# Forgetting attention followed by a spectral mix on one core: the output stage's steps, its GpSimd blocks and its stores are reordered

## The chip, the core and the metric

The kernel runs on one core of one Trainium2 chip. The metric is the time of one execution on the device in microseconds (us), as the median of the runs; lower is better. Engines are named as the profile names them: PE is TensorE's matmul, PEld its weight load, DVE is VectorE, ACT is ScalarE, POOL is GpSimd, and SP is SyncE, whose queue issues the stores of the result.

## The reference

Eight batches, eight heads, 576 positions, 64 values a head, 64 spectral modes; all inputs and the result are float32.

```python
# attention with a forgetting gate
scores = q @ k.T / 8;  cum = cumsum(log(clip(f, 1e-4, 1)))
attn   = softmax(causal(scores + cum[:, :, :, None] - cum[:, :, None, :]))
x      = (attn @ v)            # regrouped to (8, 576, 512)
# spectral mix
X = rfft(x, axis=1)            # the first 64 modes are kept
Y[:, m] = X[:, m] @ (w_r[m] + 1j * w_i[m])     # 64 complex matrices of 512 x 512
y = irfft(Y, n=576, axis=1)
u = x + y
out = u + maximum(u @ w_ch, 0)                 # (8, 576, 512)
```

## The kernel before

**Stages.** The first stage runs the attention of 32 pairs of heads and transforms each pair into the frequency domain. The second stage streams the 64 pairs of mode matrices through TensorE in 16 groups of four modes and, between the transfers, prepares for every batch the product of `x` with `w_ch` (`XW`) and folds the first 48 modes into both `x_all` (which becomes the base of `u`) and `XW` (which becomes the base of `z = u @ w_ch`). The last stage, the output stage, is what the change touches. It starts when the last four modes are known.

**What the output stage makes.** The result has 8 batches of 576 rows, taken as four blocks of 128 rows and one of 64. Two batches form a pair `p`. A step makes two result blocks of 128 x 512 float32 (256 KB each), called n = 0 and n = 1 here. An ordinary step takes one block of 128 rows of both batches of a pair. The last 64 rows of the two batches of one pair fit together into one block of 128 rows, so a joined step makes the 64-row ends of two pairs, which are four batches. There are 16 ordinary and 2 joined steps, 36 blocks, 9.44 MB. The list `steps` (L647 to L651) gives the order: before, pair 0, the joined step of pairs 0 and 1, pair 1, pair 3, the joined step of pairs 2 and 3, pair 2. The joined steps are therefore numbers 4 and 13 of 0 to 17.

**One block.** `base` (L857) puts the prepared part into a bank of PSUM with one matmul by the identity per block (`base_mm`, L657): for U from `x_all`, for Z from `XW`. `rest` (L867) adds the last 16 modes of each batch with one short matmul per block (L877), from `yl`, which holds 32 rows for each of four batches. An ordinary matmul of `rest` uses 32 of the array's rows, a joined one 64. ACT copies U from PSUM to the tile `u_sb` (`copy_u`, L907 to L912). Then DVE makes the result block, `max(Z, 0) + u_sb`, in one instruction (L944).

**Help from GpSimd.** In the steps of `by_pool` the block n = 1 is not made on DVE: ACT writes `Relu(Z)` (L941) and GpSimd adds `u_sb` (L942). In the steps of `late_x` the matmul that puts `x_all` into U is left out for n = 1, and GpSimd adds `x_all` to the finished block (L949).

**The last modes.** `yl[h]` is made by `last_modes(h)` (L885 to L905) for batches 0 to 3 (h = 0, ahead of step 0) and 4 to 7 (h = 1): eight matmuls, then one copy on ACT (L904) and one on DVE (L905). `turn` is the iteration in whose beginning the second call stands. It also decides the banks: PSUM has eight, two in `psT`, two in `psA` and four in `psX`. Until the turn Z has `psX` and U changes between `psT` and `psA`; after it U has `psX` and Z changes between the other two. So each of U and Z is double buffered.

**The order in iteration i.** Instructions stand on each engine in the order of the program. PE has the base of U of step i + 1, the base of Z of step i, the `rest` of U of step i + 1 and the `rest` of Z of step i. ACT copies U of step i + 1. Then the two blocks of step i are made and stored.

**Stores.** The list `held` collects finished blocks, and SP issues them (L963), the last one appended first. Steps 0 to 7 and the last one are `alone`: each block is stored by itself, and where GpSimd works on n = 1, that store is held back until n = 0 of the next step has been made, and stands behind it. The other ordinary steps store both blocks in one transfer of 512 KB, when both are ready. A result tile `o_sb` holds the two blocks of a step; there are seven of them.

Of the kernel before, what the change touches and what calls it, by code (L numbers as in the profile page):

```python
# [13 lines left out]
ALU = mybir.AluOpType  # L14
ACT = mybir.ActivationFunctionType
# [8 lines left out]
def kernel(  # L24
# [11 lines left out]
    nc = tc.nc  # L36
# [586 lines left out]
    with ExitStack() as bctx:  # L623
# [15 lines left out]
        psT = bctx.enter_context(tc.tile_pool(name="psT", bufs=2, space=PSUM))  # L639
        psA = bctx.enter_context(tc.tile_pool(name="psA", bufs=2, space=PSUM))  # L640
        psX = bctx.enter_context(tc.tile_pool(name="psX", bufs=4, space=PSUM))

        def bank(where, name):
            return where.tile([128, D], F32, tag={id(psT): "t", id(psA): "a", id(psX): "x"}[id(where)], name=name)

        last64 = NSB - 1
        steps = []  # L647
        for p0, p1 in ((0, 1), (3, 2)):
            steps += [[(p0, sb), (p0, sb)] for sb in range(last64)]
            steps += [[(min(p0, p1), last64), (max(p0, p1), last64)]]  # L650
            steps += [[(p1, sb), (p1, sb)] for sb in range(last64)]  # L651

        def base_mm(ps, n, k, which, stop=False):

# [188 lines left out]
                            )  # L843

        usb = bctx.enter_context(tc.tile_pool(name="usb", bufs=6))
        by_pool = (2, 6, 9, 14)
        late_x = (3, 5, 7, 8, 10, 11, 12, 15, 16)
        turn = 7
        yl = {}

        def parts(n):
# [5 lines left out]
        def base(n, which):  # L857

            wide = n < turn if which else n > turn
            where = psX if wide else (psT, psA)[n % 2]  # L860
            ps = [bank(where, "UZ"[which]) for _ in range(2)]
            for k in range(2):
                if which or not k or n not in late_x:
                    base_mm(ps[k], n, k, which)
            return ps

        def rest(n, which, ps):  # L867

            for b, k, sb in parts(n):
                r = (b + 2 * which) % 4  # L870
                if sb < last64:
                    grp = slice(32 * r, 32 * r + 32)
                    lhsT = BI4[grp, sb * 128 : sb * 128 + 128]
                else:
                    grp = slice(32 * r, 32 * r + 64)
                    lhsT = BI4_il[grp, :, :].rearrange("p i j -> p (i j)")
                nc.tensor.matmul(  # L877
                    ps[k][:],
                    lhsT=lhsT,
                    rhs=yl[b // 4][which][grp, :],  # L880
                    start=bool(k) and not which and n in late_x,
                    stop=True,
                )

        def last_modes(h, py, pyw):  # L885

            for eb in range(NEB):
                nc.tensor.matmul(
                    py[:, eb * 128 : (eb + 1) * 128],
                    lhsT=YLa[h][:, eb, :, :].rearrange("p b c -> p (b c)"),  # L890
                    rhs=ident_bf[:, :],
                    start=True,
                    stop=True,
                )
            for eb in range(NEB):
                nc.tensor.matmul(
                    pyw[:],
                    lhsT=YLw[h][:, eb, :, :].rearrange("p b c -> p (b c)"),
                    rhs=wch[:, eb, :],
                    start=(eb == 0),  # L900
                    stop=(eb == NEB - 1),
                )
            yl[h] = [ylpool.tile([128, D], BF16, tag="yl", name="yl") for _ in range(2)]
            nc.scalar.copy(yl[h][0][:], py[:])  # L904
            nc.vector.tensor_copy(yl[h][1][:], pyw[:])  # L905

        def copy_u(n, U):  # L907

            us = [usb.tile([128, D], F32, tag="usb", name="u_sb") for _ in range(2)]
            for k in range(2):  # L910
                nc.scalar.copy(us[k][:], U[k][:])
            return us  # L912
# [5 lines left out]
        u_next = copy_u(0, U0)  # L918
        held = []
        for i in range(len(steps)):  # L920
            if i == turn:
                last_modes(1, bank(psT, "pyl"), bank(psT, "pywl"))
            more = i + 1 < len(steps)
            if more:
                U = U1 if i == 0 else base(i + 1, 0)
            Z = Z0 if i == 0 else base(i, 1)
            if more:
                rest(i + 1, 0, U)
            rest(i, 1, Z)
            u_now = u_next  # L930
            if more:
                u_next = copy_u(i + 1, U)
            o_sb = wpool.tile([128, 2, D], F32, tag="w8", name="o_sb")
            p, sb = steps[i][0]
            s0 = sb * 128
            split, late = i in by_pool, i in late_x
            alone = i < 8 or i == len(steps) - 1
            for n in range(2):
                u_sb = u_now[n]
                if split and n == 1:  # L940
                    nc.scalar.activation(o_sb[:, n, :], Z[n][:], ACT.Relu)  # L941
                    nc.gpsimd.tensor_tensor(o_sb[:, n, :], o_sb[:, n, :], u_sb[:], ALU.add)  # L942
                else:
                    nc.vector.scalar_tensor_tensor(  # L944
                        o_sb[:, n, :], Z[n][:], 0.0, u_sb[:], ALU.max, ALU.add
                    )
                if late and n == 1:
                    ov = o_sb[:, n, :].rearrange("p (g c) -> p g c", g=NEB)
                    nc.gpsimd.tensor_tensor(ov, ov, x_all[:, :, 2 * p + n, sb, :], ALU.add)  # L949
                if sb == last64:  # L950
                    b0 = 2 * steps[i][n][0]
                    held.append((out[b0 : b0 + 2, s0:S, :].rearrange("b p e -> p b e"), o_sb[:, n, :]))
                elif alone:
                    held.append((out[2 * p + n, s0 : s0 + 128, :], o_sb[:, n, :]))
                elif n == 1:
                    held.append(
                        (out[2 * p : 2 * p + 2, s0 : s0 + 128, :].rearrange("b p e -> p b e"), o_sb[:])
                    )
                if alone and n == 1 and (split or late):
                    break  # L960
                while held:
                    to, frm = held.pop()
                    nc.sync.dma_start(to, frm)  # L963
# [30 lines left out]
```

## Time and profile before

| | |
|---|---|
| median of 3 runs | 437.77 us (437.42 to 439.06) |
| profiled execution, time | 440.27 us |
| profiled execution, span from first to last instruction | 438.5 us |
| granted TensorE clock, mean over the span | 0.938 |
| output stage, from its first store's issue to the last instruction | 408.99 to 438.5 us |
| stores | 20 of 256 KB and 8 of 512 KB |

The span is what the profile's views show; 1.77 us of the profiled execution lie outside it. Each row of a group or of the timeline names the line of the kernel, the engine, the operation and `out<-in` with shapes. In the view of stretches each row gives the length, the busy time of the five engines with their instruction counts, the granted clock, the mean busy share of the 16 DMA engines and what they moved in GB/s. In the view of waits a row gives the waiting queue, what released it, the total, the count and the longest wait.

### The profile page before, as it was taken

The page shows a single profiled execution, that of the slowest core. Times are in us where ns is not written, and L with a number is a line of the kernel's source. Part 1 is how long each engine was busy: PE and PEld are TensorE (multiplying, and loading weights), DVE is VectorE, ACT ScalarE, POOL GpSimd, SP SyncE. Part 2 cuts the span into 40 slices and gives each one's busy share as a digit, 9 for nine tenths or more (in the row PEclk, how much of TensorE's full clock was granted, in tenths as well). Part 3 has the DMA queues.
Part 4 walks back from the last instruction along what each step waited for, and adds up shares of the span by engine and source line. Part 5 has one row for each costly group of instructions (what it writes and reads, how often), then busy time and mean ns, then how long its engine had stood idle before and what let it go on. Part 6 is the DMA issues. An engine that isn't in the chain of part 4 may idle for free.

```text
span 438.5 us, 10295 instructions
## 1 busy us (share of the span) xinstructions
PE 348.4 (79%) x4264; PEld 191.7 (44%) x4274; DVE 268.0 (61%) x650; ACT 234.8 (54%) x359; POOL 146.1 (33%) x216
## 2 busy tenths in 40 slices
PE   1589877798988988989896484699888598889993
PEld 0355555555555555555563242243333233335330
DVE  4677888867788778888885231222233166455784
ACT  4455776777877756566561022034132166355883
POOL 6454444444544444344214111111122212100283
PEclk9999999999999999999999588599699599699998
DMA  8999999999999999999999999999999999995598
GB/s 180 205 232 221 230 222 232 228 230 228 230 231 224 228 223 227 224 224 223 230 215 212 212 212 212 213 211 212 212 211 212 210 209 210 210 210 106 193 341 331
DMA packets 68414, 96.75 MB, mean 221 GB/s; under 512 B 3600, under 2 KB 45072, under 8 KB 68368
## 3 DMA queue, kind: packets, MB, share of 16 engines
q0 software_dynamic: 62800, 85.64, 105.5%
q1 hardware_dynamic: 5568, 10.47, 6.6%
q8 instruction: 33, 0.54, 0.5%
q14 instruction: 13, 0.11, 0.1%
HBM read 163.73 MB, written 9.44 MB: 395 GB/s over the span
## 4 chain that ended last, share of the span: by engine, by line
PE 40%; DMA 32%; DVE 19%; ACT 3%; issue 3%; POOL 1%; POOLq 0%; ACTq 0%; DVEq 0%
DMA w<-in_moe_w_i_dram 22%; DMA w<-in_moe_w_r_dram 8%; PE pav L477 6%; DVE vT L384 5%; DVE qkT L360 5%; PE A L194 5%; DVE x_all L492 4%; PE pd L521 4%; PE sps L432 4%; PE tv L382 3%; PE vp L393 3%; DMA qk<-in_k_dram 2%; PE U L657 2%; PE s L423 2%; ACT e L426 2%
## 5 line engine op out<-in xcount | busy, mean ns | idle before, releaser
L439 ACT ACTIVATE et<-sps 128x1024 bf16<-128x1024 f32 x96 | 96.0, 1049 | 15.8 <-PE sps L432 12.8
L477 PE MATMUL pav<-vs,et 128*128 128x65 bf16 (+1 forms) x896 | 52.7, 200 | 0.2 <-DVE vn L372 0.2
L360 DVE COPY qkT<-tp 128x640 bf16<-128x640 bf16 x64 | 48.8, 764 | 4.8 <-PE tp L355 4.7
L818 DVE TENSOR_TENSOR Yb<-A,yx 128x512 bf16<-128x512 f32 x15 | 10.4, 691 | 61.6 <-PE A L194 61.6
L477 PEld LDWEIGHTS <-et 128*128 128x128 bf16 (+1 forms) x896 | 37.6, 104 | 18.2 <-issue 13.7
L432 PE MATMUL sps<-qkT 64*128 64x512 bf16 (+4 forms) x320 | 40.3, 315 | 1.1 <-DVE qkT L360 1.1
L697 PE MATMUL pxw<-wch,xT 128*128 128x512 bf16 (+1 forms) x152 | 39.5, 405 | 1.0 <-DVE xT L687 0.4
L194 PE MATMUL A<-w,XP 128*16 128x512 bf16 (+1 forms) x240 | 22.2, 453 | 21.8 <-DMA w<-in_moe_w_i_dram 14.1
L355 PE MATMUL tp<-ident_bf,qk 128*64 128x128 bf16 x576 | 30.6, 238 | 10.9 <-DMA qk<-in_k_dram 10.9
L492 DVE TENSOR_TENSOR x_all<-pav,rcp 128x384 bf16<-128x384 f32 (+2 forms) x96 | 36.2, 377 | 3.3
L384 DVE COPY vT<-tv 128x576 bf16<-128x576 bf16 x32 | 24.2, 757 | 19.7 <-PE tv L382 19.7
L165 POOL DMA_DIRECT2D w<-in_moe_w_r_dram x16 | 11.9, 742 | 70.6 <-PE A L194 50.8
L156 POOL DMA_DIRECT2D w<-in_moe_w_r_dram x27 | 20.4, 757 | 39.9 <-PE A L194 9.1
L704 ACT CAST XW<-pxw 128x512 bf16<-128x512 f32 (+1 forms) x16 | 9.3, 584 | 45.6 <-PE pxw L697 26.6
L404 ACT COPY vs<-vp 128x576 bf16<-128x576 bf16 x32 | 20.5, 639 | 21.9 <-PE vp L400 21.9
L704 ACT CAST yx<-pxw 128x512 bf16<-128x512 f32 (+1 forms) x24 | 14.0, 584 | 32.8 <-PE pxw L697 32.8
L109 POOL DMA_DIRECT2D qk<-in_q_dram x32 | 19.5, 611 | 35.1 <-DMA w<-in_moe_w_r_dram 8.4
L165 POOL DMA_DIRECT2D w<-in_moe_w_i_dram x19 | 13.3, 697 | 52.4 <-PE A L194 23.8
L744 ACT CAST x_all<-pu 128x512 bf16<-128x512 f32 (+1 forms) x40 | 23.4, 584 | 10.6 <-PE pu L743 9.8
L491 DVE RECIPROCAL rcp<-pav 128x6 f32<-128x6 f32 (+2 forms) x96 | 16.2, 169 | 17.7 <-PE pav L477 17.6
L156 POOL DMA_DIRECT2D w<-in_moe_w_i_dram x27 | 20.3, 752 | 18.5 <-DMA w<-in_moe_w_i_dram 8.0
L355 PEld LDWEIGHTS <-qk 128*64 128x64 bf16 x576 | 19.7, 117 | 14.8 <-issue 9.6
(149 smaller groups left out, 685.3 us busy)
## 6 DMA issues: line engine op xcount, KB each, us to landing
w<-in_moe_w_r_dram POOLq DMA_DIRECT2D x16, 1024.0 KB, 29.8
w<-in_moe_w_i_dram POOLq DMA_DIRECT2D x15, 1024.0 KB, 32.4
w<-in_moe_w_r_dram POOLq DMA_DIRECT2D x27, 512.0 KB, 10.9
w<-in_moe_w_i_dram POOLq DMA_DIRECT2D x27, 512.0 KB, 12.4
vt<-in_v_dram POOLq DMA_DIRECT2D x29, 288.0 KB, 10.6
out_dram<-o_sb SPq DMA_DIRECT2D x20, 256.0 KB, 3.2
qk<-in_q_dram POOLq DMA_DIRECT2D x32, 144.0 KB, 10.8
qk<-in_k_dram POOLq DMA_DIRECT2D x32, 144.0 KB, 10.6
```

The lines of the kernel that those rows point to most:

```text
L156: nc.gpsimd.dma_start(w8[:, t, :, :], src[4 * u : 4 * u + 4, dc * 128 : (dc + 1) * 128, :].rearrange("m p e -> p m e"),)
L165: nc.gpsimd.dma_start(w8[:, j : j + step, :, :].rearrange("p m r e -> p m (r e)"), src[m : m + step, 256:512, :].rearrange("m (p r) e -> p ...
L194: nc.tensor.matmul(A[32 * j : 32 * j + M, :], lhsT=lhsT, rhs=rhs, start=st_, stop=sp_)
L355: nc.tensor.transpose(tp[64 * hp : 64 * hp + 64, r - r0, :, :].rearrange("p n c -> p (n c)"), qk[:, hp, r * 64 : r * 64 + 64], ident_bf[:, :],
L360: nc.vector.tensor_copy(st[i]["T"][:].rearrange("p n (c r) -> p n c r", r=9)[:, :, :, r0:r1], tp[:, 0 : r1 - r0, :, :].rearrange("p r n c ...
L384: nc.vector.tensor_copy(st[i]["vT"][:].rearrange("p (c r) -> p c r", r=9), tv[:].rearrange("p r c -> p c r"))
L432: nc.tensor.matmul(ps[:, hp, c : c + n], lhsT=KT[sl, jb * 128 : jb * 128 + 128], rhs=QT[sl, i0 : i0 + n], start=True, stop=True,)
L439: nc.scalar.activation(st[i]["et"][:, T, :, :], ps[:], ACT.Exp, scale=scale)
L477: nc.tensor.matmul(pav[:Ms, sb % 3, hp, :], lhsT=eblk(i, hp, jb, sb), rhs=rhs, start=(jb == 0), stop=(jb == sb),)
L492: nc.vector.tensor_tensor(x_all[:ns, g, b, lo:hi, :].rearrange("p s (h d) -> p s h d", h=2), pav[:ns, lo % 3 : lo % 3 + n, :, 0:Dh], _stri ...
L697: nc.tensor.matmul(pxw[rows, :], lhsT=xT[:, eb, sb * 128 : sb * 128 + Ms], rhs=wch[:, eb, :], start=(eb == 0), stop=(eb == NEB - 1),)
L744: nc.scalar.copy(x_all[rows, :, to, sb, :], pu[rows, :].rearrange("p (g c) -> p g c", g=NEB))
```

## The change

The joined steps move from numbers 4 and 13 to the two ends, 0 and 17. The pairs between them keep their order (0, 1, 3, 2). GpSimd makes block n = 1 of three steps instead of four (2, 8 and 15 instead of 2, 6, 9 and 14), and there Relu comes ahead of the copies of the next U on ACT. `late_x` has nine steps as before, others in part. Every block is stored by itself in all steps, so there are 36 stores. The last modes of batches 4 to 7 are made at iteration 8 instead of 7, in the banks of `psA` instead of `psT`; step 9, the first that reads them, has its U in that same iteration.

```diff
-        steps = []
-        for p0, p1 in ((0, 1), (3, 2)):
-            steps += [[(p0, sb), (p0, sb)] for sb in range(last64)]
-            steps += [[(min(p0, p1), last64), (max(p0, p1), last64)]]
-            steps += [[(p1, sb), (p1, sb)] for sb in range(last64)]
+        steps = [[(p, sb), (p, sb)] for p in (0, 1, 3, 2) for sb in range(last64)]
+        steps = [[(0, last64), (1, last64)]] + steps + [[(2, last64), (3, last64)]]
...
-        by_pool = (2, 6, 9, 14)
-        late_x = (3, 5, 7, 8, 10, 11, 12, 15, 16)
-        turn = 7
+        by_pool = (2, 8, 15)
+        late_x = (3, 5, 6, 9, 10, 11, 12, 13, 14)
+        turn = 8
...
             if i == turn:
-                last_modes(1, bank(psT, "pyl"), bank(psT, "pywl"))
+                last_modes(1, bank(psA, "pyl"), bank(psA, "pywl"))
...
             u_now = u_next
-            if more:
-                u_next = copy_u(i + 1, U)
             o_sb = wpool.tile([128, 2, D], F32, tag="w8", name="o_sb")
             p, sb = steps[i][0]
             s0 = sb * 128
-            split, late = i in by_pool, i in late_x
-            alone = i < 8 or i == len(steps) - 1
+            if i in by_pool:
+                nc.scalar.activation(o_sb[:, 1, :], Z[1][:], ACT.Relu)
+                nc.gpsimd.tensor_tensor(o_sb[:, 1, :], o_sb[:, 1, :], u_now[1][:], ALU.add)
+            if more:
+                u_next = copy_u(i + 1, U)
             for n in range(2):
-                u_sb = u_now[n]
-                if split and n == 1:
-                    nc.scalar.activation(o_sb[:, n, :], Z[n][:], ACT.Relu)
-                    nc.gpsimd.tensor_tensor(o_sb[:, n, :], o_sb[:, n, :], u_sb[:], ALU.add)
-                else:
+                if i not in by_pool or n == 0:
                     nc.vector.scalar_tensor_tensor(
-                        o_sb[:, n, :], Z[n][:], 0.0, u_sb[:], ALU.max, ALU.add
+                        o_sb[:, n, :], Z[n][:], 0.0, u_now[n][:], ALU.max, ALU.add
                     )
...
-                elif alone:
+                else:
                     held.append((out[2 * p + n, s0 : s0 + 128, :], o_sb[:, n, :]))
-                elif n == 1:
-                    held.append(
-                        (out[2 * p : 2 * p + 2, s0 : s0 + 128, :].rearrange("b p e -> p b e"), o_sb[:])
-                    )
-                if alone and n == 1 and (split or late):
+                if n == 1 and (i in by_pool or i in late_x):
                     break
                 while held:
                     to, frm = held.pop()
```

More of the change, by code (lines that the diff above doesn't have):

```diff
@@ L935 @@
             s0 = sb * 128
-            split, late = i in by_pool, i in late_x
-            alone = i < 8 or i == len(steps) - 1
-            for n in range(2):
-                u_sb = u_now[n]
-                if split and n == 1:
-                    nc.scalar.activation(o_sb[:, n, :], Z[n][:], ACT.Relu)
-                    nc.gpsimd.tensor_tensor(o_sb[:, n, :], o_sb[:, n, :], u_sb[:], ALU.add)
-                else:
+            if i in by_pool:
[3 more added lines that the diff above has]
+                u_next = copy_u(i + 1, U)
+            for n in range(2):
+                if i not in by_pool or n == 0:
                     nc.vector.scalar_tensor_tensor(
-                        o_sb[:, n, :], Z[n][:], 0.0, u_sb[:], ALU.max, ALU.add
+                        o_sb[:, n, :], Z[n][:], 0.0, u_now[n][:], ALU.max, ALU.add
                     )
-                if late and n == 1:
+                if i in late_x and n == 1:
                     ov = o_sb[:, n, :].rearrange("p (g c) -> p g c", g=NEB)
```

## The prediction

> **What bounds the kernel now.** I read the page first, for the span and the stores, then the trace only from the point where the last modes are known, since all that the change touches comes after it.
>
> ```profile
> span 438.5 us, 10295 instructions
> out_dram<-o_sb SPq DMA_DIRECT2D x20, 256.0 KB, 3.2
> ```
>
> Next, the busy time by stretches of the output stage; the last two columns are the busy share of the DMA engines and their GB/s.
>
> ```profile
> 409.00:410.00 1.00, 1.00 (x8) 0.31 (x7) 0.78 (x2) 0.77 (x2) 0.00 (x0) 1.00 0.15 53
> ...
> 413.00:414.00 1.00, 1.00 (x7) 0.40 (x7) 0.89 (x3) 0.85 (x3) 0.88 (x2) 1.00 0.44 156
> 414.00:415.00 1.00, 1.00 (x9) 0.25 (x7) 1.00 (x2) 0.51 (x2) 0.94 (x1) 1.00 0.76 281
> 415.00:416.00 1.00, 1.00 (x11) 0.26 (x7) 0.93 (x3) 0.95 (x2) 0.00 (x0) 1.00 0.89 326
> 416.00:421.00 5.00, 4.95 (x35) 1.86 (x33) 4.32 (x8) 4.65 (x10) 3.58 (x3) 1.00 1.02 377
> 421.00:422.00 1.00, 1.00 (x8) 0.29 (x7) 0.60 (x2) 1.00 (x3) 0.92 (x1) 1.00 0.65 242
> 422.00:423.00 1.00, 1.00 (x8) 0.19 (x7) 0.99 (x2) 1.00 (x3) 0.86 (x2) 1.00 0.52 195
> 423.00:424.00 1.00, 1.00 (x5) 0.23 (x4) 1.00 (x3) 1.00 (x3) 1.00 (x2) 1.00 0.83 311
> 424.00:437.00 13.00, 6.87 (x39) 1.93 (x38) 7.45 (x12) 6.02 (x12) 6.58 (x6) 0.94 1.03 378
> 437.00:438.00 1.00, 0.00 (x0) 0.00 (x0) 0.00 (x0) 0.00 (x0) 0.00 (x0) 0.50 0.06 18
> ```
>
> The result is 9.44 MB. At the 378 GB/s of the long row that takes 25.0 us, or 0.69 to 0.70 us for each of 36 blocks. The first packet moves at about 409.86 (53 GB/s is 0.14 of a full us) and the last at about 437.05: 27.2 us. So the transfers lack work for about 2.2 us, and the rows say where: 0.59, 0.26 and 0.14 us in 413 to 416 (one minus the row over 378), which I call the first gap, 0.99; 0.36, 0.48 and 0.18 in 421 to 424, the second gap, 1.02; the rest is scattered. From 424 on the transfers never lack work, though PE has stopped by 431 and the last result instruction ends by 432.7. **The stores' stream bounds the stage. Only two things can move the end: the time of the first store, and the gaps.** The most that can be gained with the first store where it is, is 2.2 us.
>
> The waits of the queue that issues the stores say what makes the second gap:
>
> ```profile
> SPq L963 <- POOL o_sb L949: 5.5, 7, 1.2
> SPq L963 <- POOL o_sb L942: 1.7, 2, 0.9
> ```
>
> From step 8 on a store carries both blocks, so a finished n = 0 waits for GpSimd's n = 1. Steps 8 to 12 all have GpSimd in them, at 1.16 us (L949) or 1.27 (L942) after DVE's or ACT's part. The first gap comes from PE, as the timeline shows:
>
> ```profile
> 411.62 0.39 PE L877 MATMUL U<-yl,BI_il 64*128 64x512 bf16 x2
> ...
> 411.94 0.39 PE L877 MATMUL Z<-yl,BI 32*128 32x512 bf16 x2
> ...
> 412.42 4.64 DVE L944 SCALAR_TENSOR_TENSOR o_sb<-Z,u_sb 128x512 f32<-128x512 f32 x7 [0.74 <-PE Z L877]
> ```
>
> In ordinary iterations the four short matmuls of `rest` start within 0.01 us of each other (two at 410.32, two at 410.33); beside a joined step's U, Z's pair starts 0.32 later. DVE waits 0.74 for it, the next store comes late, and the queue has run dry.
>
> **The change part by part.** *Joined steps to the ends.* Before, four iterations mix a joined pair with an ordinary one, at 0.32 us of PE each: 3, 4, 12 and 13. After, only the first and the one before last do. At the first it should cost nothing: there U's pair already starts at 407.60 and Z's at 407.80, because Z waits for DVE's copy of `yl` (L905). The bounds are 0 and 0.32, which would put the first store and the end later; I take 0. At the end the stores' backlog (437.05 less 432.7, over 4 us) hides it. In iteration 3 Z's pair then starts at 411.62 instead of 411.94, DVE at about 412.10 instead of 412.42, and the store behind it 0.32 earlier.
>
> *Relu ahead of the copies, three blocks instead of four.* Relu of step 2 ran at 411.70 behind two copies; ahead of them it can run at about 410.85, when its Z is ready. GpSimd's block is then done near 412.8 instead of 413.67, and no longer stands behind n = 0 of step 3. The price is that the copies of U for step 3 start 0.6 us later, at 411.4: the first is done by 412.0, just before DVE needs it at 412.10, and PE's next use of that bank is at about 412.05. Zero, with 0.3 as the bound, three times. One block more on DVE is 0.63 us (six take 3.78 in the trace at 428.83); as DVE ends four microseconds before the stores, that is hidden, and would cost its 0.63 if it weren't.
>
> *Other steps in `late_x`.* The count stays nine, so PE saves as many matmuls as before. From one iteration's `rest` to the next it takes 1.08 us with one base matmul of U (409.24 to 410.32, 414.63 to 415.71) and 1.30 with two (417.88 to 419.17). GpSimd has eight operations in a row at steps 8 to 15, at 1.16 to 1.28 each, against about 1.26 of DVE for a step's two blocks and 1.40 of transfer: it keeps up.
>
> *Every block by itself.* n = 0 goes out when DVE has made it, and a late n = 1 follows behind n = 0 of the next step, about 0.6 us later. SP issues 36 stores instead of 28. An issue takes 0.33 to 1.15 us, median 0.38, and the long ones stand where the queue is full. What does a store cost by itself? The stretch 416 to 421 holds single blocks alone and moves 377 GB/s, 424 to 437 holds mostly double ones and moves 378. So I take 0 for eight more, with bounds of 0 and 0.33 each.
>
> The Trainium skill, in "DMA: Bandwidth & Descriptors", section "Bandwidth", speaks against this edit: it advises batches of at least 1 MiB to reach three quarters of the peak, and its fit gives every transfer a fixed 2.0 us besides its bytes. By that rule eight more transfers, one after the other, would be an estimated 16 us. The two rows just named do not agree with it here.
>
> *The last modes at iteration 8.* The eight matmuls run 416.03 to 417.13 on PE and the copies take 0.61 (ACT) and 0.69 (DVE). Before, the first reader came an iteration later. After, it is in the same iteration: PE goes from the matmuls through three base matmuls (0.65) to a `rest` that waits for ACT's copy, with whatever ACT has ahead of it (two copies of U, 1.07). I expect up to 0.3 us of waiting there, and 0.4 of DVE after it, since step 9's Z needs the `psA` banks that DVE's copy of `yl` must first empty and DVE has just one block (step 8 is one of GpSimd's) to fill the time.
>
> Is there cover? From 412.10 DVE has work without a break: steps 3 to 7 at 1.26 each end at 418.4, the copy of `yl` at 419.1, n = 0 of step 8 at 419.8, of step 9, with the 0.4, at 420.8, of step 10 at 422.05. The transfers, restarted at about 414.0 with block 5 and taking 0.70 each, are ready for these three (blocks 16, 17 and 19) at 421.7, 422.4 and 423.8, and a store needs about 0.87 from issue to its first packet (408.99 to 409.86). So each is issued 0.7 to 1.1 us before it is needed. **That is enough, but little, and it replaces the second gap by none.** The stall at this turn costs its 0.7 us if the cover is gone.
>
> *The sum.* Second gap closed: 1.02, bounds 0 and 1.02. Of the first gap 0.32, by which block 5 is issued earlier, and the 0.14 of 415 to 416, where DVE is then ahead: 0.46, bounds 0 and 0.99. That first gap has another cause as well, which stays: the list of DMA queues for 410 to 420 has one instruction fetch there, at 0.8% of 16 engines' 10 us, so some 1.3 us of one engine, and a store spreads over all of them. Together 1.5 us. The profiled execution would take 440.27 - 1.5 = 438.8; the median was 2.5 below that execution, and as the stage is at a clock of 1.00 and bound by its stores in both, I take the same 1.5 from it: 437.77 - 1.5 = 436.3 us. A measurement of this kernel can tell about 0.5%, 2.2 us, from no change, so this is a real but barely visible gain.
>
> **Rivals.** *Both gaps close wholly*, because block 5's issue, which now comes behind the fetch, gets past it: 437.77 - 2.2 = 435.6. For it: two engines (DVE and PE) have over 4 us in hand at the end. Against it: the fetch is not touched by the edit. 12%.
>
> *The hole only moves.* The turn has lost its spare iteration, so the wait of PE for ACT and of step 9's Z for the banks empties the queue at steps 8 to 10 again, where the cover is only 0.7 to 1.1; and the first gap stays with its fetch. Then nothing is gained: 437.8. For it: the second gap of before follows the same eight matmuls (PE's `rest` at 415.71, then only at 417.88). Against: singly stored blocks of DVE no longer wait behind GpSimd. 22%.
>
> *Single stores cost something.* Every store pays for its issue in the stream, by 0.33 us, the shortest issue of the trace. Eight more cost 2.6, against 1.5 gained: 438.9, slower than before. It decides from 0.19 us a store (1.5 over 8); to be 0.5% slower takes 0.46. For it: issues of up to 1.15. Against: 377 and 378 GB/s, above. 6%. The rule of the Trainium skill named above is this rival at 2.0 us a store, an estimated 452; I give it none of the chance beyond these 6%, on the same two rows.
>
> **How the numbers follow.** The forecast, 436.3, has 60%. Its own bounds reach from 435.6 (both gaps) to 437.3 (the second gap closed by half). The range runs from 435.4, the full gain with 0.2 us of scatter, to 438.2, the hole moved plus the spread of the runs above their median in part (they go to 439.06). Faster by over 0.5% means under 435.6: half of the first rival, and one part in ten of the forecast by scatter, 12%. Slower by over 0.5% means over 440: a little of the third rival and what I have not seen, 4%. The rest, 84%, is within 0.5%.
>
> **What would show it.** Right: in the stretch 421 to 424 the share of the DMA engines is 1.0; the first issue is still near 409.0; DVE starts step 3 near 412.1; SP's waits for GpSimd fall under 3 us in total; DVE ends by 431.5; the last packet is near 435.6. Wrong: a dip below 0.9 in 418 to 425 behind the eight matmuls (the second rival), 0.73 us or more for a block in stretches without a dip (the third), a first store after 409.3, or a changed stage ahead of 408.

## The result

The changed kernel takes 437.17 us (median of 22 runs, 436.0 to 438.08), the kernel before 438.0 in the same comparison (22 runs, 437.25 to 439.45). The ratio is 0.9976, with a 95% interval of 0.9967 to 0.9984: about 1.05 us less (0.7 to 1.45; the two medians differ by 0.83). The gain is smaller than the 1.5 forecast, and 437.17 lies within the stated range.

The two profiled executions differ by 3.9 us in span (438.5 and 434.6), but most of that lies ahead of the change: the first DVE instruction that closes the last modes starts at 405.30 before and at 402.60 after. So all profiles here are compared **from that instruction (YLa, L806 or L803) to the end of the span**, which I call the stage: 33.2 us before, 32.0 after, 1.2 less. Since every stage length comes from one profiled execution, it is read beside the timed comparison.

The stretches of the changed kernel, columns as before; a time here corresponds to one 2.7 us later in the kernel before.

```profile
span 434.6 us, 10304 instructions
out_dram<-o_sb SPq DMA_DIRECT2D x36, 256.0 KB, 3.2
```

```profile
407.00:408.00 1.00, 1.00 (x8) 0.25 (x7) 0.91 (x3) 1.00 (x2) 0.00 (x0) 1.00 0.27 98
...
411.00:412.00 1.00, 1.00 (x8) 0.31 (x7) 1.00 (x3) 0.91 (x3) 0.99 (x1) 1.00 0.86 311
412.00:413.00 1.00, 1.00 (x9) 0.28 (x7) 1.00 (x2) 0.79 (x2) 0.00 (x0) 1.00 0.80 295
413.00:418.00 5.00, 4.83 (x31) 1.85 (x33) 4.22 (x8) 4.11 (x9) 3.12 (x3) 1.00 1.04 382
418.00:421.00 3.00, 3.00 (x21) 0.74 (x18) 3.00 (x6) 3.00 (x7) 2.17 (x3) 1.00 1.03 386
421.00:432.00 11.00, 6.43 (x39) 1.84 (x35) 7.33 (x12) 5.79 (x12) 6.43 (x6) 0.99 1.03 383
432.00:433.00 1.00, 0.00 (x0) 0.00 (x0) 0.00 (x0) 0.00 (x0) 0.00 (x0) 0.50 0.92 340
433.00:434.00 1.00, 0.00 (x0) 0.00 (x0) 0.00 (x0) 0.00 (x0) 0.00 (x0) 0.50 0.03 10
```

The second gap is gone: none of the rows from 413 to 432 is under 1.03. The first gap has shrunk from 0.99 to 0.42 us (one minus 311 and 295 over 383). But the first packet moves at 407.74, 5.14 us into the stage; before it was at 409.86, 4.56 into it. The last moves at 433.03. **The stream became 1.9 us shorter and started 0.6 us later.** The waits of SP's queue answer to those shown of before:

```profile
SPq L953 <- POOL o_sb L943: 0.6, 1, 0.6
SPq L953 <- POOL o_sb L933: 0.4, 1, 0.4
```

GpSimd made the stores wait 7.2 us before and 1.0 after. And this, from the timelines, is the late start; first the kernel before, then the changed one:

```profile
405.30 0.29 DVE L806 TENSOR_TENSOR YLa<-AT,accT 128x128 bf16<-128x128 f32 x1 [1.32 <-PE AT L211]
...
408.27 1.29 DVE L944 SCALAR_TENSOR_TENSOR o_sb<-Z,u_sb 128x512 f32<-128x512 f32 x2 [0.52 <-PE Z L877]
...
408.99 0.35 SPq L963 DMA_DIRECT2D out_dram<-o_sb  x1
```

```profile
402.60 0.29 DVE L803 TENSOR_TENSOR YLa<-AT,accT 128x128 bf16<-128x128 f32 x1 [1.80 <-PE AT L211]
...
404.90 0.39 PE L874 MATMUL U<-yl,BI 32*128 32x512 bf16 x2
405.22 0.39 PE L874 MATMUL Z<-yl,BI_il 64*128 64x512 bf16 x2
405.71 2.07 DVE L938 SCALAR_TENSOR_TENSOR o_sb<-Z,u_sb 128x512 f32<-128x512 f32 x3 [0.66 <-PE Z L874]
406.44 0.63 SPq L953 DMA_DIRECT2D out_dram<-o_sb  x1
```

The first result instruction of DVE starts 2.97 us into the stage before and 3.11 after, since Z's joined matmuls follow U's by 0.32 (before by 0.20). The first store is then issued at 408.99 and at 406.44. Its first packet follows 0.87 us later before and 1.30 after. The joined store takes 0.63 us to issue where the ordinary one took 0.35.

### The profile page after: what moved, and what is told of

It is laid out like the page before. It is cut to its first block, busy times and chain, and to the rows that moved or that the text cites. A ratio compares the mean times of both kernels' runs of the same rounds, so it can differ in the third digit from the quotient of the medians.

```text
span 434.6 us, 10304 instructions
## 1 busy us (share of the span) xinstructions
PE 343.3 (79%) x4264; PEld 189.6 (44%) x4274; DVE 267.9 (62%) x651; ACT 234.1 (54%) x358; POOL 145.0 (33%) x215
## 3 DMA queue, kind: packets, MB, share of 16 engines
HBM read 163.73 MB, written 9.44 MB: 398 GB/s over the span
## 4 chain that ended last, share of the span: by engine, by line
DMA 43%; PE 31%; DVE 18%; issue 3%; ACT 3%; POOL 1%; DVEq 0%; POOLq 0%
DMA w<-in_moe_w_r_dram 22%; DMA w<-in_moe_w_i_dram 20%; PE pav L477 5%; DVE vT L384 4%; DVE qkT L360 4%; DVE x_all L492 4%; PE A L194 4%; PE sps L432 3%; PE tv L382 3%; PE pd L521 3%; PE vp L393 2%; DMA qk<-in_k_dram 2%; PE Z L654 2%; DVE vn L372 2%; PE U L654 2%
## 5 line engine op out<-in xcount | busy, mean ns | idle before, releaser
L701 ACT CAST yx<-pxw 128x512 bf16<-128x512 f32 (+1 forms) x24 | 14.0, 585 | 31.4 <-PE pxw L694 31.4
L109 POOL DMA_DIRECT2D qk<-in_q_dram x32 | 19.5, 610 | 32.5 <-PE sps L432 6.2
L109 POOL DMA_DIRECT2D qk<-in_k_dram x32 | 19.2, 601 | 19.3 <-DMA w<-in_moe_w_i_dram 5.2
```

The lines of the kernel that those rows point to most:

```text
L109: nc.gpsimd.dma_start(qk[64 * n : 64 * n + 64, :, :], src[b, 2 * g : 2 * g + 2, :, :].rearrange("h (p r) d -> p h (r d)", p=64),)
```

## The experiments

Stage lengths are differences of two times of the trace, the end of the span less the start of the first YLa instruction. The gap lengths are from the stretches, as above.

**Single stores alone (s_only), joined steps at the ends alone (j_only), the change with double stores again (a_pair), the joined steps both last (o_first).**

```diff
 s_only, on the kernel before
-            alone = i < 8 or i == len(steps) - 1
+            alone = True
 j_only, on the kernel before
-        steps = []
...
+        steps = [[(p, sb), (p, sb)] for p in (0, 1, 3, 2) for sb in range(last64)]
+        steps = [[(0, last64), (1, last64)]] + steps + [[(2, last64), (3, last64)]]
 a_pair, on the changed kernel
+            alone = i < 8 or i == len(steps) - 1
...
-                else:
+                elif alone:
                     held.append((out[2 * p + n, s0 : s0 + 128, :], o_sb[:, n, :]))
+                elif n == 1:
+                    held.append(
+                        (out[2 * p : 2 * p + 2, s0 : s0 + 128, :].rearrange("b p e -> p b e"), o_sb[:])
+                    )
-                if n == 1 and (i in by_pool or i in late_x):
+                if alone and n == 1 and (i in by_pool or i in late_x):
 o_first, on the changed kernel
-        steps = [[(0, last64), (1, last64)]] + steps + [[(2, last64), (3, last64)]]
+        steps = steps + [[(0, last64), (1, last64)], [(2, last64), (3, last64)]]
-        by_pool = (2, 8, 15)
-        late_x = (3, 5, 6, 9, 10, 11, 12, 13, 14)
-        turn = 8
+        by_pool = (1, 7, 14)
+        late_x = (2, 4, 5, 8, 9, 10, 11, 12, 13)
+        turn = 7
-                last_modes(1, bank(psA, "pyl"), bank(psA, "pywl"))
+                last_modes(1, bank(psT, "pyl"), bank(psT, "pywl"))
```

> The kernel before with one edit: every block is stored by itself. Theory (the stores' stream sets the end; double stores waiting for GpSimd made the second gap): no stretch from 8 us after the start of the first L806 instruction on with the transfers under 0.9 busy, except the first gap, which stays; from the first L806 instruction to the last instruction 32.2 instead of 33.2 us; the time about 1.0 us less than before. Rival (the gain came from the order of the steps, single stores bring nothing): 33.2 us and the time of before. Second rival (a store has a price of its own, 0.33 us): 35 us or more.

> The kernel before with one edit: the joined steps stand first and last. Theory: the first packet comes 0.5 to 0.6 us later, counted from the first L803 instruction (5.1 instead of 4.5 us), the first gap shrinks by about 0.5 us, the second stays; 33.0 to 33.4 us from the first L803 instruction to the end, the time within 0.3 us of before. Rival (the order of the steps is what gained): about 32.0 us and 1.0 less than before.

> The changed kernel with one part undone: steps 8 to 16 store both blocks in one transfer of 512 KB again. Theory: steps 9 to 14 all wait for GpSimd at n = 1 before they store, and a gap of 0.5 to 1.0 us comes back behind the last modes; 32.5 to 33.0 us from the first L80x instruction to the end against 32.0, the time 0.5 to 1.0 us above the changed kernel's. Rival (the gap was made by the place of the last modes or by the joined steps, not by the stores): 32.0 us, the changed kernel's time.

> The changed kernel with both joined steps at the end (numbers 16 and 17), all other steps one number earlier, the last modes at iteration 7 in psT. Theory (the joined step at the front puts the first packet off by 0.58 us, 0.14 by Z's short matmuls and 0.44 by the store's longer issue): the first packet 4.5 us after the first L803 instruction instead of 5.1, the first store's issue 0.35 us long instead of 0.63, about 31.4 us to the end instead of 32.0, the time 0.5 to 0.6 us under the changed kernel's. Rival (the late first packet is a chance of that one execution, or is hidden): 5.1 or 4.5 us with no difference to the end, the changed kernel's time.

| | ratio to the kernel before, 95% | stage |
|---|---|---|
| s_only | 0.9977 (0.9961 to 0.9993) | 32.5 |
| j_only | 0.9984 (0.9970 to 0.9998) | 32.8 |
| a_pair | 0.9991 (0.9973 to 1.0008) | 32.6 |
| o_first | 0.9976 (0.9964 to 0.9987) | 31.8 |

The intervals of these four ratios overlap, so the times alone do not tell the four apart; the stages and their stretches do.

*s_only* gains 0.7 us of stage instead of 1.0. Its stretches, with the first gap in 411 to 414 as before:

```profile
411.00:412.00 1.00, 1.00 (x7) 0.29 (x6) 0.95 (x2) 0.85 (x3) 0.92 (x1) 1.00 0.64 236
412.00:413.00 1.00, 1.00 (x8) 0.31 (x7) 0.94 (x2) 0.75 (x2) 0.96 (x1) 1.00 0.83 301
413.00:414.00 1.00, 1.00 (x11) 0.26 (x7) 0.93 (x2) 0.71 (x2) 0.19 (x1) 1.00 0.63 236
414.00:426.00 12.00, 11.95 (x73) 3.84 (x74) 10.18 (x18) 10.64 (x21) 9.43 (x8) 1.00 1.02 379
426.00:427.00 1.00, 1.00 (x8) 0.24 (x7) 0.65 (x2) 1.00 (x3) 0.00 (x0) 1.00 0.85 311
```

The second gap (421 to 424 before, about 419.3 to 422.3 here) lies inside the long row at 1.02: it is closed by this edit alone. The first gap is as long as before (236, 301 and 236 against 379 make 0.96 us), and a new small one of 0.18 stands at 426, where DVE was 0.65 busy and waited 0.4 us for a copy of U; that is most of what is short of the 1.0. That the joined step in the middle makes this wait was not tested. A price of 0.33 per store is excluded.

*j_only* has the late first packet (first store issued at 407.41, two in 1.26 us, as in the changed kernel), and its first gap shrinks although Relu is still behind the copies:

```profile
412.00:413.00 1.00, 1.00 (x8) 0.28 (x7) 0.96 (x2) 0.68 (x3) 1.00 (x1) 1.00 0.83 299
413.00:414.00 1.00, 1.00 (x9) 0.31 (x8) 0.96 (x2) 1.00 (x3) 0.09 (x1) 1.00 0.87 320
```

Against the 379 of its long row that is 0.37 us, no more than the 0.42 of the changed kernel. So the joined steps' place, not Relu's, is what the first gap needed. Its stage is 0.4 shorter, a little better than expected; its time is 0.7 us less (0.1 to 1.3), where at most 0.3 was expected. SP still waits 8.8 us for GpSimd there, and the second gap stays: 272, 168 and 365 GB/s in 419 to 422, 0.88 us. The 0.7 of *s_only* and the 0.4 of *j_only* make up the 1.1 of the whole change.

*a_pair* brings that gap back, in the changed order, with the SP queue waiting 7.1 us for GpSimd:

```profile
419.00:420.00 1.00, 1.00 (x9) 0.31 (x7) 1.00 (x3) 1.00 (x3) 0.27 (x2) 1.00 0.86 322
420.00:421.00 1.00, 1.00 (x8) 0.31 (x7) 1.00 (x2) 1.00 (x3) 1.00 (x1) 1.00 0.86 326
421.00:422.00 1.00, 1.00 (x7) 0.13 (x6) 1.00 (x3) 0.92 (x3) 0.90 (x2) 1.00 0.62 234
```

DVE is fully busy in these rows, and from 417 to 422.5 SP waits 3.4 us for GpSimd and 0.6 for DVE: finished blocks n = 0 stand behind GpSimd's n = 1. The stage is 0.6 longer than the changed kernel's; the timed ratio, 0.9991, points the same way, though its interval overlaps that of the changed kernel.

*o_first* starts as expected. Its first block is an ordinary one, whose store is issued in 0.35 us, and the first packet comes 4.55 us into the stage:

```profile
406.56 0.35 SPq L953 DMA_DIRECT2D out_dram<-o_sb  x1
```

It gained 0.3 of the 0.6 us that the start gave; the queue ran dry for a moment at 409 to 410 (225 GB/s, 0.41 us). I put this down to GpSimd's first step, now number 1, which leaves the early stores one DVE block short; in o2 below, where that step is number 2 again, the row 409 to 410 moves 387 GB/s. In time o_first equals the changed kernel.

**Where the rest of the first gap comes from.** In the changed kernel the rest is 0.42 us at 411 to 413, and DVE is fully busy in both rows. The list of DMA queues for 410 to 412 names another candidate:

```profile
q1 hardware_dynamic: 377, 0.68, 92.2%
q8 instruction: 1, 0.02, 2.9%
```

One packet of queue q8 takes 2.9% of 16 engines' 2 us, 0.93 us of one engine; in the trace it starts 7.74 us into the stage, at 410.34. The page of the profile counts 33 such packets and 0.54 MB, 16 KB each. I take them for PE's instruction fetch, and moved it by making some of the short matmuls that turn `Yb` (L818 of the changed kernel) twice, long before the stage, where PE waits for weights:

```diff
-                for eb in range(NEB):
+                for eb in [e % NEB for e in range(2 * NEB if u < NX else NEB)]:                # 96 instructions more
+                for eb in [e % NEB for e in range(NEB + (NEB if u < 5 else 2 * (u == 5)))]:   # 44 more
```

The first line made a_pad (on the changed kernel), b_pad (on the kernel before) and o2_pad. o2 is o_first with `by_pool` and `late_x` as in the changed kernel.

> The changed kernel; in the first twelve groups of modes the four short matmuls that turn Yb (L818) are made twice, where PE waits for weights anyway. That is 96 more instructions of PE, and puts the fetch of PE's last 16 KB of instructions 96 instructions earlier, to about the first L803 instruction, before the first store. Theory (what is left of the first gap and the late end of the last block are the fetch, which takes one DMA engine for 0.94 us 7.7 us after the first L803 instruction): the gap at 9.1 to 9.4 us (0.36) and the thin last half us (0.28) go; 31.4 us from the first L803 instruction to the end instead of 32.04, the time 0.6 us less. Rival (the gap is DVE's and PE's supply): 32.0 us, the same time.

> The kernel before with the same 96 instructions more. Theory: block 5's issue is not held back by the fetch, 0.33 us instead of 0.65, so the first gap (0.74 us at 8.0 to 8.8 us after the first L806 instruction) shrinks by 0.3, but Z of step 3 still comes 0.32 late and the second gap stays; 32.7 to 32.9 us to the end instead of 33.16. Rival (the first gap is the fetch alone): it goes whole, 32.3. Second rival (the fetch does nothing): 33.2.

> Both joined steps at the end as in o_first, but GpSimd's steps at 2, 8, 15 and late_x numbered as in the changed kernel, last modes at iteration 7. Theory (o_first lost 0.35 us at 6.6 us because step 1 gave only one block to the first stores): that hole goes, the hole of the fetch at about 9 us stays; 31.4 us from the first L80x instruction to the end instead of 31.8 (o_first) and 32.04 (the changed kernel). Rival (the early start only empties the queue elsewhere): 31.8.

> o2 with the 96 instructions more. Theory: first packet at 4.55 us, 36 blocks at 0.69 us without a hole, 1.35 us from the last packet to the end: 30.7 to 30.9 us instead of 31.4, and the time some 2.3 us (0.5%) less than the kernel before. Rival (supply and not the fetch sets the holes): 31.4.

| | ratio to the kernel before, 95% | stage | without the 96 |
|---|---|---|---|
| a_pad | 0.9989 (0.9977 to 1.0002) | 32.7 | 32.0 |
| b_pad | 1.0025 (1.0013 to 1.0037) | 34.3 | 33.2 |
| o2_pad | 1.0011 (0.9999 to 1.0022) | 32.9 | 32.3 |
| o2 | 0.9976 (0.9964 to 0.9989) | | 32.3 |

All four expected stage lengths were missed, and the misses were useful. With 96 more instructions the fetch did move ahead of the stores, but the next one, which I had thought lay behind the end, came into the middle of them. In a_pad's stretches:

```profile
409.00:424.00 15.00, 14.82 (x94) 4.75 (x92) 13.73 (x23) 13.45 (x28) 9.48 (x8) 1.00 1.03 381
...
425.00:426.00 1.00, 1.00 (x9) 0.23 (x7) 1.00 (x3) 0.87 (x2) 0.96 (x2) 1.00 0.97 358
426.00:427.00 1.00, 1.00 (x10) 0.34 (x6) 0.95 (x2) 0.86 (x2) 1.00 (x2) 1.00 0.46 166
...
434.00:435.00 1.00, 0.00 (x0) 0.00 (x0) 0.00 (x0) 0.00 (x0) 0.00 (x0) 0.50 0.29 102
```

The first row is the half of a_pad's theory that held. Its earlier fetch is over 0.6 us into the stage, long before the first store, and from 409 to 424 the transfers run at 381 GB/s without a hole. So the 0.42 us that was left of the first gap is the fetch, and not a lack of blocks.

The next fetch starts at 424.3 (4.6% of 16 engines' 2 us in the list for 424 to 426, 1.5 us). SP's issue that stands beside it lasts from 424.49 to 426.13, 1.64 us, the longest of that stretch. Then 0.57 us of transfer is missing (166 against 383), with DVE and GpSimd busy, and the stream ends on a thin row, 102 GB/s. In the changed kernel the issue beside the fetch is 1.11 us long. In twelve of the fourteen traces an issue that runs beside a fetch ends 0.30 to 0.44 us after the fetch does; in the other two (s_only, b_pad) no issue beside it is stretched. My reading is that a store spreads over all engines, that the one that fetched is behind, that SP cannot issue further ahead of it, and that it ends last; what in the queue holds SP, no run here shows.

In o2 the fetch (3.3% of 16 engines' 3 us, 1.58 us) fell earlier in the stream, and the rows 410 to 412 move 240 and 43 GB/s: 1.3 us are missing, which is more than the early start had brought. Not all of that is the fetch. o2_pad has the same order with the fetches elsewhere, one from 0.45 us ahead of the stage and one 21.3 us into it, and still lacks 0.46 us at 411 to 412 and 0.35 at 417 to 418:

```profile
411.00:412.00 1.00, 1.00 (x11) 0.29 (x7) 1.00 (x3) 1.00 (x3) 0.57 (x1) 1.00 0.56 205
417.00:418.00 1.00, 1.00 (x7) 0.26 (x6) 0.85 (x2) 1.00 (x3) 0.36 (x1) 1.00 0.67 248
```

There the queue waits for DVE; the second hole stands behind the last modes, which o2 makes at iteration 7. For the first hole an estimate from the traces says why: five blocks at 0.69 us from the first packet at 4.54 last until 8.0; the sixth store is issued 7.73 us into the stage, and its first packet needs some 0.87 more. In the changed kernel the five blocks start at 5.12 and last until 8.6, and the sixth store is issued at 7.58: just in time. So in this order an earlier start mostly empties the queue earlier.

**44 instructions more, and the turn.**

```diff
 a_turn7, on the changed kernel
-        turn = 8
+        turn = 7
-                last_modes(1, bank(psA, "pyl"), bank(psA, "pywl"))
+                last_modes(1, bank(psT, "pyl"), bank(psT, "pywl"))
```

> The changed kernel with 44 instructions of PE more (22 of the short L818 matmuls made twice, in the first six groups of modes) instead of 96. In the runs so far a fetch of 16 KB came about every 250 instructions of PE: with none more at 201 instructions before the end (7.7 us after the first L803 instruction), with 96 more at 308 and again at 48 (20.6 us). With 44 more the first should come some 250 before the end, 2.5 to 4 us after the first L803 instruction and so ahead of the stores, and the next should fall behind the end. Theory (a fetch within the stream of stores costs 0.6 to 1.3 us, in a hole and in one engine that ends last): no hole and no thin end; 31.3 to 31.5 us to the end instead of 32.0 (none more) and 32.7 (96 more), the time 0.5 to 0.7 us under the changed kernel's. Rival (the extra instructions themselves cost): between 32.0 and 32.7.

> The kernel before with the 44 instructions more. Theory: no fetch in the stream; the first gap shrinks from 0.74 to about 0.45 (Z of step 3 is still 0.32 late), the second stays, no thin end: 32.7 to 32.9 us from the first L806 instruction to the end instead of 33.16 (none more) and 34.3 (96 more). Rival (the first gap is the fetch alone): 32.3.

> o2 (both joined steps at the end, first store early) with the 44 instructions more. Theory: first packet at 4.55 us, at most 0.4 us of holes, 36 blocks at 0.69 us, 1.35 to the end: 30.7 to 31.2 us instead of 32.3 (o2), and 2.0 to 2.4 us less time than the kernel before. Rival (an earlier start only empties the queue earlier): 31.4 or more, no better than the changed kernel with the same 44.

> The changed kernel with the last modes at iteration 7 in psT again, an iteration ahead of their first reader. Theory: DVE's idle time at the turn (0.23 and 0.54 us in the changed kernel's trace) moves or shrinks, and the transfers, which are covered there, do not see it: 32.0 us from the first L803 instruction to the end, the changed kernel's time within 0.2 us. Rival (the turn's place mattered): 31.5 or less, or 32.5 or more.

| | ratio to the kernel before, 95% | stage |
|---|---|---|
| a_p44 | 0.9973 (0.9961 to 0.9986) | 32.0 |
| b_p44 | 0.9994 (0.9986 to 1.0003) | 33.1 |
| o2_p44 | 0.9964 (0.9950 to 0.9977) | 32.0 |
| a_turn7 | 0.9969 (0.9957 to 0.9981) | 32.0 |

The single fetch came where it was meant to: it starts 3.4 to 4.2 us into the stage, and there is no second one. What the 96 had added is gone, and 44 extra instructions by themselves cost nothing that shows. But the expected 31.4 did not come. The changed kernel's gap at its old place is closed, and another opened at the start:

```profile
409.00:410.00 1.00, 1.00 (x8) 0.41 (x8) 1.00 (x3) 0.94 (x3) 0.00 (x0) 1.00 0.72 258
410.00:412.00 2.00, 2.00 (x14) 0.43 (x12) 1.51 (x3) 2.00 (x6) 1.27 (x1) 1.00 0.93 344
412.00:414.00 2.00, 2.00 (x13) 0.62 (x11) 2.00 (x5) 1.91 (x5) 1.15 (x1) 1.00 1.03 383
```

(a_p44; its first packet is at 409.2, 5.1 us into the stage.) The fetch runs from 4.15 to 5.08 us into the stage, so it is over before the first packet, but not before the second store's issue: that one runs beside it, from 4.51 to 5.47, 0.96 us instead of 0.61. It is the same long issue at another place. *o2_p44*, expected at 30.7 to 31.2, ended its stage no sooner than a_p44, although its first packet came 0.58 us earlier, at 4.54. The issue of its second store runs beside the fetch too, and there are holes again in 408 to 410 (254 and 307 GB/s) and 417 to 418 (260). The rival, that the early start only empties the queue earlier, came nearer than the theory.

The kernel before answers its own question: with the fetch out of the stream (b_p44) the first gap is as long as it was.

```profile
411.00:412.00 1.00, 1.00 (x7) 0.30 (x6) 0.90 (x2) 0.85 (x2) 0.89 (x2) 1.00 0.64 240
412.00:413.00 1.00, 1.00 (x8) 0.29 (x6) 0.99 (x2) 0.71 (x2) 1.00 (x1) 1.00 0.85 315
413.00:414.00 1.00, 1.00 (x11) 0.31 (x7) 0.93 (x3) 0.75 (x2) 0.14 (x1) 1.00 0.56 209
```

That is 0.37, 0.17 and 0.45 (one minus the row over 378), 0.98 us in all. So before, the gap was the joined step in the middle (j_only), and the fetch was not needed for it. What is left of it after the change does follow the fetch's place (a_pad).

*a_turn7* gives the changed kernel's stage, 32.0, as expected; DVE's waits at the turn are 0.5 and 0.4 us. It and o2_p44 have the lowest ratios, but their intervals overlap that of the changed kernel, so **no version was shown to beat it.**

## Why the prediction was right in sign and size class, and where its sum was off

**What bounds the stage: right.** The stores' stream ends the kernel in every run, and the parts of the stage add up: 4.56 us to the first packet, 27.2 of stream and 1.45 behind it before; 5.14, 25.3 and 1.57 after.

**Second gap closed, 1.02: right, by the named cause.** Single stores alone close it (s_only), double ones reopen it (a_pair).

**First gap, 0.46 of 0.99: 0.57 measured, with the wrong reason for the remainder.** I held the fetch for a second cause of the gap before the change. b_p44 shows that it was not; the fetch costs what is left after the change, since a_pad, with the fetch elsewhere, has no first gap.

**Joined step at the front, "it should cost nothing", 0 with a bound of 0.32: the step that failed.** It cost 0.58 us. 0.14 is Z's matmuls, within the bound. The other 0.43 is from the store: a joined block's store was issued in 0.63 us instead of 0.35, and its first packet came 1.30 us after issue instead of 0.87. I had followed the moved step through PE, ACT and DVE, and not through the pattern of its store. o_first, whose first block is ordinary, has the early packet back. The long issues that I saw in the trace I had put down to a full queue; at the front no queue is full. The 0.58 is the delay of the first packet. What it cost at the end of the stage is less sure: o_first won back 0.3 of it, and o2_p44 none against a_p44.

**A term that was missing** went the other way: the long rows move 383 GB/s instead of 378, 24.6 us instead of 25.0 for 9.44 MB, about 0.3. No run isolates it; the rows with double stores move 378 again in a_pair. The sum by measured terms: 1.02 + 0.57 + 0.3 - 0.58 - 0.1 (more behind the last packet) = 1.2, the difference of the stages. That it came near the forecast is in part luck, since the two errors have opposite signs. The range holds the rival of the moved hole as well (437.8), so it says little that the time fell into it; what excludes that rival is the interval of the ratio, which stays under 1, and the profile.

**The turn: right.** DVE waited 0.5 us for Z ahead of step 9, where 0.4 was forecast, and idled 0.2 ahead of step 8. The wait of up to 0.3 that I forecast for PE does not show: its `rest` starts at 416.06, 0.32 after the last base matmul. The transfers at 1.04 did not see any of it, and with the turn an iteration earlier nothing changed. The hole did not move.

**A price for each store: excluded.** 36 single stores moved 383 GB/s. The Trainium skill's advice in "DMA: Bandwidth & Descriptors", section "Bandwidth", to batch to 1 MiB or more therefore did not hold for these overlapped stores of 256 KB from SP. The figures behind that advice, and the fit with the fixed 2.0 us, which stands in another section of that page, "Anatomy of one DMA — SWDGE (gpsimd) path", are given for transfers issued from GpSimd; the prediction took them for every transfer.

**Relu ahead of the copies.** DVE's step 3 started 6.87 us into the stage, against 6.80 worked out and 7.12 before; but in j_only, with Relu behind the copies, it started at 6.87 too. So the 0.25 us came from the joined steps' place, and no gain of its own was shown for Relu.

## What to carry to other kernels

Where a stage is bound by its stores, find the holes in the transfers and the moment of the first packet; everything else is cover. A finished block should not share a transfer with one that a slower engine still works on. Whatever is put first sets the first packet, here 0.58 us later with a joined block; but an earlier first packet helps only as far as the blocks behind it keep up.

## What the runs showed of the hardware

Packets of 16 KB on the queue q8 come about once in 260 instructions of PE and its weight load here (33 for the 8538 of the page of the profile) and move when PE's instruction count changes, so I take them for PE's instruction fetch. That one occupies one of the DMA engines that also carry the stores is my reading of the busy shares. In the midst of a saturated stream, 20.6 to 21.4 us into the stage, such a fetch made the stage 0.6 to 1.1 us longer (the three kernels with 96 more instructions against the same without, whose fetch lies earlier). The Trainium skill states the block of 16 KiB and 256 instructions in "Runtime: NRT & Kernel Launch", section "Instruction fetch mechanics", and calls the cost mostly hidden; the size agrees with these traces, and the cost was not hidden where the fetch fell beside the issue of a store. So a kernel that is 96 instructions longer in an early stage can end about 1 us later, which is as much as this whole change brought.
